# Masks, normalizations and feature steps shared between VectorE and GpSimd, with a new table of order, engines and buffers

## The chip, the cores and the metric

The kernel runs on one core of a Trainium2 chip, in one launch. A core has five engines that run their own instruction streams and wait for each other through semaphores: TensorE (PE in the profile, with its weight loads as PEld), ScalarE (ACT), VectorE (DVE), GpSimd (POOL) and SyncE (SP), which here only issues DMAs. The metric is the device time of one execution in microseconds, as the median of several runs.

## The reference

A sequence of 2048 tokens with 512 channels runs through four blocks, two of a kind, each with its own normalization and residual:

```python
x = x + _A_ref(_layernorm(x), A_wq, A_wk, A_wv, A_wo, A_beta)
x = x + _B_ref(_layernorm(x), B_wqkv, B_w_phi, B_wo)
x = x + _A_ref(_layernorm(x), A_wq, A_wk, A_wv, A_wo, A_beta)
x = x + _B_ref(_layernorm(x), B_wqkv, B_w_phi, B_wo)
```

Block A has 32 heads of 16 channels and works in 4 segments of 512 tokens. Inside a segment it is causal softmax attention; beside it stands a linear memory of the earlier segments, and a gate `g` per head mixes the two:

```python
phi = lambda t: jnp.where(t > 0, t + 1.0, jnp.exp(t))
logits = einsum('bhqd,bhkd->bhqk', qs, ks) * scale + mask
a_dot = einsum('bhqk,bhkd->bhqd', softmax(logits), vs)
a_mem = einsum('bhld,bhde->bhle', phi(qs), M) / (einsum('bhld,bhd->bhl', phi(qs), z)[..., None] + 1e-06)
o = g * a_mem + (1.0 - g) * a_dot
M = M + einsum('bhld,bhle->bhde', phi(ks), vs);  z = z + phi(ks).sum over l
```

Block B is linear attention without a mask: queries and keys go through a small matrix per head, then softmax of it and of its negative are the features; keys and values of all 2048 tokens are summed into one matrix per head before the queries are multiplied with it.

## The kernel before

The sequence is held in SBUF as `X`, 16 tiles of 128 tokens. The two pairs of layers (`L` = 0, 1) run one after the other. Block A goes by segment `s` (four tiles each): `a_proj` makes queries, keys and values of a segment, `a_att` does the attention of two tiles at a time, `out_proj` adds the result to `X`; then the tiles are normalized again and `b_keys` adds the segment's part of block B's sums. After the fourth segment `b_query` runs over the four groups of tiles, and in layer 0 the next layer's normalization and projections follow each group.

What the change touches is this:

- `ln` normalizes one tile: statistics (`bn_stats`, L590, and `bn_aggr`, L591, on DVE), the inverse root (L598 and L600 on POOL, or on ACT for the first four tiles), and then the normalized tile `xn`, `(X - mean) * rstd`, 128x512. `xn` is on DVE at L611, or on DVE (L607) or ACT (L608) where the tile may go either way. SP then transposes it by DMA (L383), or PE does (`tpe`).
- `a_proj` copies the keys out of PSUM (`Kev`, L374 on ACT or L375 on DVE) and writes four masked copies of them (`Km`, L703), 128x1024 each: a mask keeps one head in four and sets the others to zero, so that a matmul over 64 rows, which hold four heads, sees one head at a time. There are 64 such masks in the program, all on DVE. The score matmuls of block A read them as tile `pQ`.
- `phi` makes the feature map: ACT takes the exponential, L649 takes `max(x, 0) + 1`, L650 the minimum of the two. There are 24 of each, the latter two on DVE.
- Two kinds of additions, L882 (attention plus memory) and L1093 (the two halves of block B's result), are on DVE or POOL by the table.

Nothing of the order is decided when the program is built. Every operation is recorded in a graph with the engines that may do it and a cost in ns for each. A packed table, `ORDER`, holds three lists: the sequence of all 2748 operations, the engine of each, and the buffer of each of the 1498 tiles. `place` unpacks it and `emit` writes each engine's stream in that sequence, with the waits that the data and the reuse of buffers need. An engine never takes its operations in another order. So the costs in the code are notes for whoever made the table; they do nothing at run time.

Of the kernel before, what the change touches and what calls it, by code (L numbers as in the profile page):

```python
# [10 lines left out]
ALU = mybir.AluOpType  # L11
# [301 lines left out]
class Kernel:  # L313
# [149 lines left out]
    def T(self, pool, cls):  # L463
        return Tile(pool, cls)
# [122 lines left out]
    def ln(self, t, xT, flex=False, pe=False, root="pool"):  # L587
# [14 lines left out]
        xn = self.T(self.p1, "xn")  # L602
        if flex:
# [3 lines left out]
            self.g.op({"dve": (323, lambda e: e.tensor_scalar(xn.t[:], self.X[:, t, :], self.mv[:, t, 0:1], rs, op0=ALU.subtract, op1=ALU.mult)),  # L607
                       "act": (700, lambda e: e.activation(xn.t[:], self.X[:, t, :], ACT.Identity, scale=rs, bias=nb))},  # L608
                      [R("X", t), R("mv", t), R("rstd", t), R("nb", t)], [xn], label="xn", port=True)
        else:  # L610
          v(lambda e: e.tensor_scalar(xn.t[:], self.X[:, t, :], self.mv[:, t, 0:1], self.rstd[:, t:t + 1],  # L611
                                    op0=ALU.subtract, op1=ALU.mult), 300,
          [R("X", t), R("mv", t), R("rstd", t)], [xn], label="xn", port=True)
# [30 lines left out]
    def phi(self, dst, src):  # L644
# [4 lines left out]
        v(lambda e: e.tensor_scalar(dst.t[:], src.t[:], 0.0, 1.0, op0=ALU.max, op1=ALU.add), 335, [src[0], src[1]], [dst], label="phmax", port=True)  # L649
# [32 lines left out]
    def a_proj(self, L, s):  # L682
# [7 lines left out]
        for hp in range(2):  # L690
# [11 lines left out]
            for sl in range(4):  # L702
# [3 lines left out]
                self.g.op({"dve": (400.0, fn)}, [KT[0], KT[1], R("m4")], [KM[sl]], label="Km", port=True)  # L706
# [567 lines left out]
```

## Time and profile before

| | |
|---|---|
| time, median of 3 runs | 462.59 us (462.41 to 462.62) |
| span of the profiled execution | 461.2 us |
| instructions with a recorded time: PE, DVE, ACT, POOL | 11716, 807, 542, 160 |
| one mask, one normalization, one feature step (L649) on DVE | 476, 417, 423 ns |
| one inverse root on POOL (L598 and L600) | 272 and 587 ns |

The span runs from the first to the last instruction; the time of a run is 1.4 us more. A row of the groups of instructions gives line, engine, operation, tiles, shape and count, then the busy time of them all and the mean of one, then the idle time of the engine just before them with what ended it. Instructions of one engine overlap a little, so the busy time of a group can be less than count times mean. A row of the waits reads "engine, tile, line <- engine, tile, line that ended the wait: us in total, times, longest".

### The profile page before, as it was taken

The numbers are of one execution on the slowest core, as the hardware profiler recorded it, in microseconds if no ns is written. First come the engines' busy times: TensorE is split into PE (matmuls) and PEld (weight loads), VectorE is DVE, ScalarE is ACT, GpSimd is POOL, SyncE is SP. The second block draws the span as 40 slices with busy tenths as digits, with TensorE's granted clock in tenths as the row PEclk, the third lists the DMA queues.
The fourth block names the chain that finished last, engine by engine and source line by source line (L and its number), as shares of the span: only waits on it lengthen the run. The fifth ranks groups of instructions, "written<-read, shape, count | busy, mean of one in ns | idle before, by whom it ended". The sixth has DMA issues, their size and how long they took to land.

```text
span 461.2 us, 25354 instructions
## 1 busy us (share of the span) xinstructions
PE 437.7 (95%) x11716; PEld 295.6 (64%) x11716; DVE 416.2 (90%) x807; ACT 420.3 (91%) x542; POOL 80.1 (17%) x160
## 2 busy tenths in 40 slices
PE   8989899899999999998899999999999999998896
PEld 4456667667776776675456677677677677666553
DVE  6989998898889999898999899998899889998896
ACT  4999999899999998789699999999999999878991
POOL 2402021101221211102532031130221023110020
PEclk9999999999999999999999999999999999999999
DMA  8554642552233322100243443264113321200357
GB/s 247 127 150 80 127 63 37 75 96 54 50 46 54 46 40 36 37 3 4 48 54 78 71 85 72 49 96 61 26 39 49 50 39 27 48 14 1 50 121 180
DMA packets 90058, 30.37 MB, mean 66 GB/s; under 512 B 76640, under 2 KB 89952, under 8 KB 89952
## 3 DMA queue, kind: packets, MB, share of 16 engines
q1 hardware_dynamic: 89520, 28.48, 33.3%
q8 instruction: 92, 1.51, 1.4%
q10 hardware_dynamic: 432, 0.27, 0.2%
q14 instruction: 14, 0.11, 0.1%
HBM read 6.32 MB, written 2.10 MB: 18 GB/s over the span
## 4 chain that ended last, share of the span: by engine, by line
PE 48%; ACT 40%; DVE 6%; DMA 3%; issue 2%; SPq 0%
PE D L356 31%; ACT p L366 21%; PE D L341 15%; ACT pF L366 13%; ACT pE L366 5%; DMA p<-p 2%; PE D L662 2%; DVE X L926 1%; DMA X<-in_A_x_dram 1%; DVE p L1090 1%; DVE p L375 1%; DVE stats L590 1%; ACT pS L366 1%; DVE p L611 0%; DVE pK L375 0%
## 5 line engine op out<-in xcount | busy, mean ns | idle before, releaser
L366 ACT ACTIVATE p<-D 128x1024 bf16<-128x1024 f32 (+2 forms) x224 | 216.0, 1004 | 13.5 <-PE D L356 9.7
L366 ACT ACTIVATE pF<-D 128x896 bf16<-128x896 f32 x128 | 116.7, 940 | 2.8 <-PE D L341 2.5
L341 PE MATMUL D<-pK,pQ 64*128 64x256 bf16 (+3 forms) x1536 | 112.9, 243 | 4.1 <-ACT pF L366 1.0
L341 PEld LDWEIGHTS D<-pK,pQ 64*128 64x128 bf16 x1536 | 55.2, 94 | 40.7 <-ACT pF L366 5.4
L341 PE MATMUL D<-pV,pF 64*128 64x34 bf16 x1024 | 73.8, 175 | 0.4 <-ACT p L366 0.4
L341 PE MATMUL D<-pW,pF 64*128 64x34 bf16 x1024 | 71.3, 175 | 0.0
L341 PEld LDWEIGHTS D<-pV,pF 64*128 64x128 bf16 x1024 | 55.3, 93 | 2.3 <-ACT p L366 0.7
L341 PE MATMUL D<-pV,p 64*128 64x34 bf16 x1024 | 53.3, 176 | 0.3 <-issue 0.2
L366 ACT ACTIVATE pE<-D 128x768 bf16<-128x768 f32 x64 | 52.3, 831 | 1.4 <-PE D L341 1.0
L341 PEld LDWEIGHTS D<-pW,pF 64*128 64x128 bf16 x1024 | 51.9, 93 | 0.9
L341 PE MATMUL D<-pW,p 64*128 64x34 bf16 x1024 | 52.1, 176 | 0.0
L598 POOL TENSOR_SCALAR rstd<-mv 128x1 f32<-128x1 f32 x60 | 16.1, 272 | 205.9 <-DVE mv L591 205.5
L341 PEld LDWEIGHTS D<-pV,p 64*128 64x128 bf16 x1024 | 47.0, 93 | 3.3 <-issue 0.9
L341 PE MATMUL D<-tri,two 64*128 64x128 bf16 (+1 forms) x384 | 46.7, 234 | 0.4 <-issue 0.4
L341 PEld LDWEIGHTS D<-pW,p 64*128 64x128 bf16 x1024 | 45.2, 93 | 1.3
L590 DVE BATCH_NORM_STATS2 stats<-X 128x6 f32<-128x512 bf16 x64 | 42.9, 680 | 3.0 <-DMA X<-in_A_x_dram 2.5
L341 PE MATMUL D<-pV,pE 64*128 64x34 bf16 x512 | 44.9, 175 | 0.4 <-issue 0.4
L926 DVE TENSOR_TENSOR X<-X,D 128x1024 bf16<-128x1024 bf16 (+1 forms) x36 | 39.4, 1095 | 5.7 <-PE D L356 5.0
L341 PE MATMUL D<-pW,pE 64*128 64x34 bf16 x512 | 42.5, 175 | 0.1
L985 DVE TENSOR_REDUCE pS<-p 128x64 f32<-128x1024 bf16 (+1 forms) x36 | 38.8, 1088 | 1.8 <-ACT p L366 1.8
L375 DVE CAST p<-D 128x512 bf16<-128x512 f32 x48 | 31.1, 683 | 6.3 <-PE D L356 6.1
L356 PE MATMUL D<-WB_o,p 64*128 64x512 bf16 (+1 forms) x288 | 33.0, 353 | 2.7 <-issue 1.3
(115 smaller groups left out, 988.9 us busy)
## 6 DMA issues: line engine op xcount, KB each, us to landing
pW<-pV SPq DMA_DIRECT2D x16, 136.0 KB, 3.1
out_dram<-X SPq DMA_DIRECT2D x7, 256.0 KB, 2.8
X<-in_A_x_dram SPq DMA_DIRECT2D x3, 512.0 KB, 6.1
pX<-in_B_wqkv_dram SPq DMA_DIRECT2D x3, 512.0 KB, 4.6
p<-p SPq DMA_TRANSPOSE x76, 2.8
pX<-p SPq DMA_TRANSPOSE x54, 3.2
WA_k<-in_A_wk_dram SPq DMA_DIRECT2D x2, 256.0 KB, 6.3
WA_q<-in_A_wq_dram SPq DMA_DIRECT2D x2, 256.0 KB, 7.0
```

Of the source, the lines that this page charges most:

```text
L341: ins = e.matmul(out_ap, lhsT, rhs, start=st, stop=sp, tile_position=(basep(lhsT), basep(out_ap)))
L356: ins = e.matmul(out_ap, lhsT[64 * hf:64 * hf + 64], rhs[64 * hf:64 * hf + 64], start=k == 0 and i == 0, stop=k == 1 and i == len(lists[hf ...
L366: return self.g.op({"act": (dur, lambda e: e.activation(out_ap(), in_ap(), func, scale=scale))}, reads, writes, opens, label=label)
L375: "dve": ((340 if fast else n / 0.96 + 65), lambda e: e.tensor_copy(out_ap(), in_ap()))}
L590: v(lambda e: e.bn_stats(self.stats[:, t, :], self.X[:, t, :]), 602, [R("X", t)], [R("st", t)], label="bn")
L598: v(lambda e: e.tensor_scalar(rs, self.mv[:, t, 1:2], LN_EPS, None, op0=ALU.add), 170, [R("mv", t)], [R("rstd", t)], eng="pool", label="rstd")
L662: ins = e.matmul(D.t[c0:, r0 * 8:r0 * 8 + n], r[:, c0:], ones(r, n), start=True, stop=True, tile_position=(r0, c0))
L926: self.v(lambda e: e.tensor_tensor(X(), X(), src(), ALU.add), 65 + 512 * n / 0.96, pr + xr, xr, label="res")
L985: fn = lambda e, sgn=sgn, eo=eo, Z=Z, n=n: e.tensor_reduce(Z.t[:, 0:64 * n].rearrange("p (k s h) -> p k s h", k=n, s=2)[:, :, sgn, :], eo( ...
L1090: v(lambda e, N=N, Tm=Tm, w=w, shape=shape: e.tensor_tensor(shape(Tm.t[:]), shape(N.t[:]), w(), ALU.mult), 1131, [N, AB[(0, 0)], AB[(0, 1) ...
```

## The change

Three kinds of operations, which were bound to DVE (the normalization to DVE or ACT in some tiles), may also be on POOL. The table is a new one. The costs noted for two of them are 323 for 300 and 396 for 400 ns.

```diff
         xn = self.T(self.p1, "xn")
+        nrm = lambda e: e.tensor_scalar(xn.t[:], self.X[:, t, :], self.mv[:, t, 0:1], rs, op0=ALU.subtract, op1=ALU.mult)
         if flex:
...
-            self.g.op({"dve": (323, lambda e: e.tensor_scalar(xn.t[:], self.X[:, t, :], self.mv[:, t, 0:1], rs, op0=ALU.subtract, op1=ALU.mult)),
+            self.g.op({"dve": (323, nrm), "pool": (700.0, nrm),
                        "act": (700, lambda e: e.activation(xn.t[:], self.X[:, t, :], ACT.Identity, scale=rs, bias=nb))},
...
-          v(lambda e: e.tensor_scalar(xn.t[:], self.X[:, t, :], self.mv[:, t, 0:1], self.rstd[:, t:t + 1],
-                                    op0=ALU.subtract, op1=ALU.mult), 300,
-          [R("X", t), R("mv", t), R("rstd", t)], [xn], label="xn", port=True)
+            self.g.op({"dve": (323, nrm), "pool": (700.0, nrm)}, [R("X", t), R("mv", t), R("rstd", t)], [xn], label="xn", port=True)
...
-        v(lambda e: e.tensor_scalar(dst.t[:], src.t[:], 0.0, 1.0, op0=ALU.max, op1=ALU.add), 335, [src[0], src[1]], [dst], label="phmax", port=True)
+        fn = lambda e: e.tensor_scalar(dst.t[:], src.t[:], 0.0, 1.0, op0=ALU.max, op1=ALU.add)
+        self.g.op({"dve": (335.0, fn), "pool": (1100.0, fn)}, [src[0], src[1]], [dst], label="phmax", port=True)
...
-                self.g.op({"dve": (400.0, fn)}, [KT[0], KT[1], R("m4")], [KM[sl]], label="Km", port=True)
+                self.g.op({"dve": (396.0, fn), "pool": (1100.0, fn)}, [KT[0], KT[1], R("m4")], [KM[sl]], label="Km", port=True)
...
 ORDER = """
-c-rlG1GFYtlWpMm8fDwIZQHhO+qP}n=q}rAn`L%ab=S-MZdXt9|9jTVd+W_wli$7hWu9{~V#kghk(u{qfQFD5k^n<eNCu6dF*JchkQ&lJIzUJPDIpbPg!E7oN<u9FC<w
...
+c-qZ*1JotQ7Vbv*H^#PY+qP}nwr$(Cl?;MGGDyY~XPC?c<H@}4^UuV2_rAOCUF-EZr@O1VYUA5`e^tE>Kn7?CsUZ!dg+`D9QbJ;A3{4;vq=$kafB>N+6at2tPznk|5hw~tASu*>rqB#3
...
```

Unpacked, both tables hold the same 2748 operations and 1498 tiles. What changes its engine:

```
operation                           engine         count (of)
mask (Km, L703)                     DVE to POOL    45 (64)
normalization (xn, L607/L611)       DVE to POOL    45 (60 on DVE)
normalization (xn, L608)            ACT to POOL 1, ACT to DVE 1 (4 on ACT)
feature step (phmax, L649)          DVE to POOL    8 (24)
addition (L882)                     DVE to POOL 5, POOL to DVE 5 (24)
addition (L1093)                    DVE to POOL 6, POOL to DVE 1 (26)
evacuation of PSUM (L374/L375)      ACT to DVE 9, DVE to ACT 7
small set-up fills                  POOL to DVE 2, DVE to POOL 1
operations on DVE                   807 to 708
operations on POOL                  156 to 259
operations on ACT                   544 to 540
```

PE and SP keep all of theirs. The sequence is shuffled locally on all engines: half of PE's operations stay within one place of where they were, nine in ten within six. 1163 of the 1498 tiles have another buffer. Of SP's loads at the start, the one of X's last four tiles (12 to 15) goes from place 15 to place 6, and that of tiles 8 to 11 from place 7 to place 14, just ahead of the first transposes. At the end, one of the stores that stood ahead of SP's last transposes moves behind them.

More of the change, by code (lines that the diff above doesn't have):

```diff
@@ L1234 @@
[L1234 to L1235 removed]
+c-qZ*1JotQ7Vbv*H^#PY+qP}nwr$(Cl?;MGGDyY~XPC?c<H@}4^UuV2_rAOCUF-EZr@O1VYUA5`e^tE>Kn7?CsUZ!dg+`D9QbJ;A3{4;vq=$kafB>N+6at2tPznk|5hw~tASu*>rqB#3
+LUSk$m7q4%fifVWER=(~&;nXQD`*Xsp$fEtw$KjRLkH*xouD&xfvQjpibFLh0rj9f<OKuup#oHg8W03$;4I{UC^!ZAp(}KQ2B6^rT!ij03^GCl#03XEpcf>9WH1wk!z@tH6Z*qB_y|6R
```

110 lines of the change are left out of this document (52 added, 58 removed).

## The prediction

> **What bounds the kernel now.** I read the page's first part, then the same busy times by stage (the windows view), because a share over the whole span is a mean over stages with different limits. A row of that view has the stretch, its length, the busy time (and the count of instructions) of PE, PEld, DVE, ACT and POOL, the granted clock, the DMA share and the GB/s.
>
> ```profile
> PE 437.7 (95%) x11716; PEld 295.6 (64%) x11716; DVE 416.2 (90%) x807; ACT 420.3 (91%) x542; POOL 80.1 (17%) x160
> 0.00:30.00 30.00, 26.79 (x360) 14.12 (x360) 24.49 (x66) 21.86 (x35) 8.89 (x32) 1.00 0.72 197
> 30.00:180.00 150.00, 143.62 (x4374) 102.18 (x4368) 136.62 (x255) 147.19 (x179) 21.55 (x40) 1.00 0.37 62
> 180.00:207.00 27.00, 26.93 (x574) 18.73 (x570) 24.40 (x47) 20.49 (x27) 3.20 (x8) 1.00 0.10 19
> 207.00:228.00 21.00, 17.54 (x543) 10.30 (x537) 18.87 (x40) 18.72 (x34) 8.13 (x12) 1.00 0.12 25
> 228.00:240.00 12.00, 12.00 (x146) 5.61 (x140) 11.90 (x22) 9.46 (x14) 4.32 (x5) 1.00 0.24 49
> 240.00:390.00 150.00, 147.91 (x4316) 104.64 (x4314) 137.25 (x268) 148.29 (x183) 27.27 (x52) 1.00 0.36 58
> 390.00:424.00 34.00, 34.00 (x720) 23.17 (x716) 31.64 (x55) 28.30 (x36) 4.31 (x9) 1.00 0.11 22
> 424.00:461.20 37.20, 28.87 (x738) 16.90 (x732) 31.03 (x59) 26.03 (x40) 2.43 (x2) 0.98 0.50 109
> ```
>
> The reader is to see that DVE, the engine that the change relieves, is the tight one almost nowhere. In the two attention stages (30 to 180 and 240 to 390, together 300 us) ACT is idle for 150 - 147.19 = 2.8 us and 150 - 148.29 = 1.7 us. In 180 to 207, 228 to 240 and 390 to 424 (73 us) PE is idle for 0.1 us in all. That leaves the start, the turn between the layers (207 to 228) and the end.
>
> Next, what PE and ACT wait for. These are the rows between 30 and 390 us in which PE's idle time ends on DVE (four more rows, one of 0.4 us at L1087 and three of 0.2 us at L375, are left out), and the one in which ACT's does:
>
> ```profile
> PE D L341 <- DVE p L1060: 1.0, 1, 1.0
> PE D L341 <- DVE p L607: 0.4, 1, 0.4
> PE D L341 <- DVE X L926: 0.4, 1, 0.4
> ...
> PE D L341 <- DVE WB_k L375: 0.2, 1, 0.2
> ACT pS L366 <- DVE pS L1061: 1.2, 1, 1.2
> ```
>
> With those four they add up to 4.2 us, and of the operations that move, one row alone is there: a normalization (L607), 0.4 us. No row names a mask (pQ, L703) or the first step of the feature map (L649). So what moves is mostly not what anyone waits for. At the turn (213 to 227) the chain of waits does run through DVE, but nearly all of it through operations that stay there (multiply L1090, residual L926, statistics L590); the normalization L607 has 3.0%, 0.4 us:
>
> ```profile
> by line: DVE p L1090 32.9%; DVE X L926 24.6%; DVE stats L590 17.6%; DVE p L1087 6.9%; DVE p L375 4.3%; DVE mv L591 3.8%; DVE p L607 3.0%; DVE pS L1065 2.9%; DVE p L1060 2.4%; DVE nb L605 2.3%; issue 1.9%; PE D L341 1.4%; DVE pS L1061 1.2%
> ```
>
> **The change, part by part.** The rows that price it:
>
> ```profile
> L703 DVE TENSOR_SCALAR pQ<-p,m 128x1024 bf16<-128x1024 bf16 x64 | 29.4, 476 | 0.5 <-ACT p L374 0.3
> L611 DVE TENSOR_SCALAR p<-X,mv,rstd 128x512 bf16<-128x512 bf16 x44 | 18.1, 417 | 1.7 <-POOL rstd L600 1.4
> L649 DVE TENSOR_SCALAR p<-p 128x1024 bf16<-128x1024 bf16 x12 | 5.0, 423 | 0.1
> 451.17 0.42 DVE L1093 TENSOR_TENSOR p<-p 128x512 bf16<-128x512 bf16 x1
> L374 ACT ACTIVATE p<-D 128x512 bf16<-128x512 f32 x28 | 15.9, 597 | 6.7 <-PE D L356 4.6 <-PE D L341 1.9
> L608 ACT ACTIVATE p<-X,nb,rstd 128x512 bf16<-128x512 bf16 x4 | 3.2, 800 | 0.0
> L518 POOL TENSOR_SCALAR_AFFINE_SELECT H<-H 128x8 f32<-128x8 f32 x1 | 0.2, 192 | 0.1
> L523 POOL TENSOR_SCALAR_AFFINE_SELECT ident<-ident 128x128 bf16<-128x128 bf16 x1 | 0.3, 292 | 0.1
> L598 POOL TENSOR_SCALAR rstd<-mv 128x1 f32<-128x1 f32 x60 | 16.1, 272 | 205.9 <-DVE mv L591 205.5
> L1093 POOL TENSOR_TENSOR p<-p x10: 1147/1154/1531, 215.2 to 443.5; 128x512 bf16<-128x512 bf16 x10
> ```
>
> *Off DVE.* The unpacked table moves 45 of 64 masks, 45 normalizations and 8 of 24 feature steps from DVE to POOL, and a net 5 additions. By busy time over count: 45 x 29.4/64 = 20.7, 45 x 18.1/44 = 18.5, 8 x 5.0/12 = 3.3, 5 x 0.42 = 2.1 us. Evacuations trade places (9 from ACT to DVE, 7 back) and one normalization comes from ACT: about +1.7 us. DVE loses 42.9 us and would stand near 373.
>
> *Onto POOL.* No row shows these three operations there. From below: one input streams from 8 to 128 elements in 292 - 192 = 100 ns, 0.83 ns an element, and the same operation on one element takes 272 ns; so 272 + 0.83 x 1024 = 1.12 us for a mask and 0.70 us for a normalization. From above: 512 elements with two inputs take 1.15 us, so 2.3 and 1.15 us. I take the lower ones, since these operations have one tensor input. POOL gains 45 x 1.12 + 46 x 0.70 + 8 x 1.12 + 5 x 1.15 = 97 us (from above 180) and stands near 177 us of 461: it does not become the bound either way.
>
> *What hides them.* A mask takes 0.6 us longer and a normalization 0.3; the rows of waits above say that nobody waited for them. Behind a normalization stands SP's transpose, and behind that the rest of SP's queue:
>
> ```profile
> SPq L383 <- DVE p L611: 36.8, 11, 10.1
> ```
>
> SP already sits up to 10.1 us there with no loss to PE, so 0.3 us more is covered; without that cover it would be 46 x 0.3 = 14 us. I cost this at 0 and keep 0 to +2.
>
> *ACT.* In the two attention stages six evacuations leave ACT and four come: 2 x 15.9/28 = **-1.1 us** on the engine that is busy 99% of that time. The bounds are 0 and -1.1 - 4.5 (all of ACT's idle time there closing too).
>
> *The turn.* One of four normalizations (800 ns) goes from ACT to POOL, but the chain there is DVE work that stays: 0, bounds -0.8 and +0.5.
>
> *The start.* The table also reorders SP's loads: the load of X's last quarter goes from behind the first four transposes to sixth place, and X's third quarter from seventh to just before the transposes.
>
> ```profile
> 14.75 6.36 SPq L383 DMA_TRANSPOSE pX<-p  x4
> 21.16 0.58 SPq L474 DMA_DIRECT2D X<-in_A_x_dram  x1
> 26.23 0.69 DVE L590 BATCH_NORM_STATS2 stats<-X 128x6 f32<-128x512 bf16 x1 [1.53 <-DMA X<-in_A_x_dram]
> 2.00:14.00 12.00, 11.41 (x161) 6.01 (x161) 9.71 (x31) 6.56 (x16) 3.62 (x12) 1.00 0.98 298
> ```
>
> DVE's idle 1.53 us ends on that late load, so it goes. In its place 4.8 MB now stand ahead of the end of X's third quarter, which at 298 GB/s lands at 2 + 16 = 18 us, about when DVE gets to its statistics: 0 to 1.5 us. I take -1.5 + 0.5 = **-1.0 us**, bounds -1.5 and +1.0.
>
> *The end.* One store fewer stands ahead of the last transposes on SP, but an addition ahead of the last one is POOL's (1.15 for 0.42 us):
>
> ```profile
> 453.12 1.19 SPq L383 DMA_TRANSPOSE p<-p  x1
> 439.57 0.57 SPq L387 DMA_DIRECT2D out_dram<-X  x1
> ```
>
> That addition started at 451.17 on DVE (quoted above); on POOL it ends at 451.17 + 1.15 = 452.3, before SP gets there: **-0.4 us** for the store, bounds -0.6 and +0.7.
>
> *A port that both engines want.* This is the term that speaks against the change.
>
> ```profile
> 130.82 1.16 POOL L882 TENSOR_TENSOR p<-p 128x512 bf16<-128x512 bf16 x1 [5.98 <-DVE p L795]
> 383.74 0.68 DVE L1007 TENSOR_TENSOR pT<-p,pT 128x1024 bf16<-128x1024 bf16 x1
> 383.91 1.53 POOL L882 TENSOR_TENSOR p<-p 128x512 bf16<-128x512 bf16 x1 [8.02 <-DVE p L795]
> 384.92 1.07 DVE L1007 TENSOR_TENSOR pT<-p,pT 128x1024 bf16<-128x1024 bf16 x1
> 220.70 1.22 DVE L1090 TENSOR_TENSOR p<-D,pS 128x1024 bf16<-128x1024 f32 x1
> 220.80 2.35 POOL L1093 TENSOR_TENSOR p<-p 128x512 bf16<-128x512 bf16 x2 [0.23 <-DVE nb L605]
> ```
>
> The first L1007 (0.68 us) runs into POOL's addition, which takes 1.53 instead of 1.16; the second starts while 0.52 us of that addition are left and takes 0.39 longer. Whoever comes second waits. L1090, which reads PSUM, and POOL's additions run side by side at full speed (1.22 us, and 2.35 us for two), so only DVE work that reads SBUF alone is hit. The Trainium skill has the rule without a price (GPSIMD Engine Reference, Key points: VectorE's SBUF interfaces are shared, and contention comes with two-port modes or two SBUF inputs); the trace agrees, with 1.07 for 0.68 us, and the rule by itself, each overlap a wait, is the port rival below. Price: after the change DVE keeps about 145 large operations that read SBUF alone (32 L1007, 24 L650, 20 L1087, 19 masks, 16 normalizations, 16 feature steps, 18 additions); POOL is on large ones for 45 x 1.12 + 46 x 0.70 + 8 x 1.12 + 26 x 1.15 = 121 us, 26% of the span. Each meets one at 0.26 and loses about 0.36 (half of a mean POOL operation of 1 us, less the 0.52 - 0.39 = 0.13 that the row above did not lose): 145 x 0.26 x 0.36 = 14 us of DVE, so DVE would show about 387 busy. DVE is 6% of the chain (below), mostly at the turn, in L1090 and L926, which read PSUM, and L590, which reads one tensor: I take 3% of the 14 us, **+0.4 us**; bounds 0 and +4 (some 30% of the 14 us on the path).
>
> ```profile
> PE 48%; ACT 40%; DVE 6%; DMA 3%; issue 2%; SPq 0%
> ```
>
> **Sum.** -1.1 - 1.0 - 0.4 + 0.4 = -2.1 us on the profiled execution's span of 461.2, so 459.1. The time runs 462.59 - 461.2 = 1.4 us above the span, so 460.5.
>
> **Rivals.** Two runs of this kernel can be told apart from about 0.2%, which is 0.9 us.
> - *The slack is used everywhere.* With 43 us less on DVE everything reaches PE and ACT earlier, and the 4.5 us that ACT is idle in the attention stages close, with the 4.2 us of waits on DVE partly among them. For it: three engines at 90% jam each other. Against it: ACT's idle time there ends on PE. -2.1 - 3.5 gives 457.
> - *It does nothing that counts.* ACT and PE hold their stages as now, the gain at the start is given back to the later quarter of X: 462.3.
> - *Slower: the port.* POOL's masks, 1.12 us each, stand before DVE's reads at places where an evacuation or a weighted value is queued behind them in DVE's order and PE waits for that. It decides as soon as more than 2.5 of the 14 us fall on the path (gain used up), and at 4 to 6 us it gives 464.5 to 466. For it: the 1.07 us above. Against it: PE and ACT wait on DVE for only 4.2 us in 360.
> - *Slower: the start.* X's third quarter lands 2 us after DVE wants it, and evacuations queue behind it: 463.8.
>
> **How the numbers follow.** Forecast (459 to 461.6) 0.37, slack used everywhere 0.12, nothing 0.24, port 0.20, start 0.07. That is faster 0.49, same 0.24, slower 0.27. Predicted: 460.5. The range takes in most of the slack case and most of the port's: 457.0 to 465.0; the forecast's own range is 459.0 to 461.6.
>
> **What would show it.** DVE near 387 us busy, POOL near 177, mask 1.1 to 1.4 us and normalization 0.7 to 0.9 on POOL; L1007 and L650 above 0.69 us on average (some near 1.1); ACT near 418 busy, still 98% and more in both attention stages; DVE's idle time on X's load gone, or moved to another quarter. The prediction is wrong if masks take 2 us (PE would wait for pQ), if the chain's DVE share grows past 10%, or if ACT's share in the attention stages falls: then PE was kept waiting by something new.

## The result, and the profile after

The changed kernel takes 545.24 us (median of 4 runs, 541.94 to 549.37), the kernel before 462.50 beside it. The ratio is 1.1786, with a 95% interval of 1.1700 to 1.1872: **slower by 18%**, 83 us, where a gain of 2 us was predicted. The profiled execution has a span of 540.2 us, which the notes below refer to.

First the page of the changed kernel: busy times, the granted clock in 40 slices, and the chain that ended last by engine.

```profile
PE 456.9 (85%) x11716; PEld 300.5 (56%) x11716; DVE 402.1 (74%) x708; ACT 422.9 (78%) x538; POOL 342.9 (63%) x263
PEclk9998989899997999899899989889799999999999
PE 34%; POOL 31%; DVE 14%; ACT 7%; DMA 7%; issue 4%; SPq 2%; DVEq 0%; POOLq 0%
```

POOL is busy for 343 us, not 177, and 31% of the chain now runs through it, where it had no share. No engine is full any more: PE fell from 95% to 85% and ACT from 91% to 78%. An engine that is busy 63% of the time and yet holds the others up doesn't lack capacity; its results come late.

The stages, in two stretches of 160 us that lie inside the two attention stages (columns as in the prediction):

```profile
40.00:200.00 160.00, 139.81 (x4038) 96.24 (x4039) 117.40 (x195) 137.56 (x165) 119.21 (x80) 0.95 0.29 52
290.00:450.00 160.00, 133.87 (x3770) 92.64 (x3770) 110.10 (x189) 128.32 (x155) 120.79 (x79) 0.95 0.30 46
```

ACT had 147.19 of 150 us in the first attention stage. Now it has 137.56 of 160, or 86%, and 80% in the second. The loss is spread over both stages; no single stall makes it.

The groups of the three operations on POOL, with the mean ns of one behind the busy time:

```profile
L703 POOL TENSOR_SCALAR pQ<-p,m 128x1024 bf16<-128x1024 bf16 x45 | 131.2, 2921 | 27.5 <-DVE p L375 13.4 <-DVE mv L591 10.3 <-ACT p L374 3.7
L603 POOL TENSOR_SCALAR p<-X,mv,rstd 128x512 bf16<-128x512 bf16 x46 | 99.3, 2161 | 7.0 <-DVE mv L591 3.3 <-DVE nb L606 0.9
L648 POOL TENSOR_SCALAR p<-pK 128x1024 bf16<-128x1024 bf16 x6 | 21.9, 3651 | 1.4 <-DVE pK L375 1.1
```

A mask takes 2.92 us where 1.12 was assumed, a normalization 2.16 for 0.70, a feature step 3.65 for 1.12. In the timeline of POOL one sees what that does to small operations that stand in the same queue (start, duration, operation, and in brackets what it waited for):

```profile
305.26 5.69 POOL L703 TENSOR_SCALAR pQ<-p,m 128x1024 bf16<-128x1024 bf16 x2 [1.96 <-ACT p L374]
311.01 3.70 POOL L648 TENSOR_SCALAR p<-pK 128x1024 bf16<-128x1024 bf16 x1
314.79 0.23 POOL L598 TENSOR_SCALAR rstd<-mv 128x1 f32<-128x1 f32 x1
314.97 1.08 POOL L600 TENSOR_TENSOR rstd<-rstd,mhalf 128x1 f32<-128x1 f32 x2
316.05 2.85 POOL L703 TENSOR_SCALAR pQ<-p,m 128x1024 bf16<-128x1024 bf16 x1
318.89 2.08 POOL L603 TENSOR_SCALAR p<-X,mv,rstd 128x512 bf16<-128x512 bf16 x1
```

An inverse root of 0.23 us comes behind 9.4 us of masks and a feature step, and the normalization that needs it stands behind one more mask on the same engine. The waits of the changed kernel name the consequences (us in total, times, longest):

```profile
POOL rstd L598 <- DVE mv L591: 68.7, 21, 11.1
ACT p L366 <- PE D L341: 41.9, 25, 4.5
...
PEld D L341 <- POOL pQ L703: 18.3, 6, 5.1
PE D L341 <- POOL pQ L703: 16.8, 6, 4.9
...
DVE p L650 <- POOL p L648: 11.5, 3, 6.1
...
DVE nb L606 <- POOL rstd L600: 8.5, 4, 4.3
...
PE D L356 <- DMA pX<-p: 6.6, 6, 3.0
```

PE waits for masks (pQ) and for late transposes, which stand behind late normalizations; DVE waits for POOL's feature steps and inverse roots. ACT then waits for PE: 41.9 us in the row on L341, which had 2.6 before. And POOL's own wait for statistics fell from 205.5 to 68.7 us: most of the slack that it had before is used up by its own work.

### The profile page after: what moved, and what is told of

It reads as the page before. It is cut to its first block, busy times and chain, and to the rows that moved or that the text cites. A ratio compares the mean times of both kernels' runs of the same rounds, so it can differ in the third digit from the quotient of the medians.

```text
span 540.2 us, 25363 instructions
## 1 busy us (share of the span) xinstructions
PE 456.9 (85%) x11716; PEld 300.5 (56%) x11716; DVE 402.1 (74%) x708; ACT 422.9 (78%) x538; POOL 342.9 (63%) x263
## 4 chain that ended last, share of the span: by engine, by line
PE 34%; POOL 31%; DVE 14%; ACT 7%; DMA 7%; issue 4%; SPq 2%; DVEq 0%; POOLq 0%
PE D L356 23%; POOL pQ L703 13%; PE D L341 11%; POOL p L603 9%; POOL p L648 5%; ACT p L366 4%; DMA pX<-p 4%; POOL rstd L600 3%; DVE X L926 2%; ACT pF L366 2%; DVE p L375 2%; DMA p<-p 2%; DMA WA_k<-in_A_wk_dram 2%; DVE stats L590 1%; SPq L474 1%
## 5 line engine op out<-in xcount | busy, mean ns | idle before, releaser
L366 ACT ACTIVATE p<-D 128x1024 bf16<-128x1024 f32 (+2 forms) x224 | 215.3, 994 | 63.1 <-PE D L341 41.9
L703 POOL TENSOR_SCALAR pQ<-p,m 128x1024 bf16<-128x1024 bf16 x45 | 131.2, 2921 | 27.5 <-DVE p L375 13.4
L341 PE MATMUL D<-pK,pQ 64*128 64x256 bf16 (+3 forms) x1536 | 116.4, 249 | 29.6 <-POOL pQ L703 16.8
L366 ACT ACTIVATE pF<-D 128x896 bf16<-128x896 f32 x128 | 114.9, 930 | 10.1 <-PE D L341 9.4
L603 POOL TENSOR_SCALAR p<-X,mv,rstd 128x512 bf16<-128x512 bf16 x46 | 99.3, 2161 | 7.0 <-DVE mv L591 3.3
L341 PEld LDWEIGHTS D<-pK,pQ 64*128 64x128 bf16 x1536 | 57.8, 96 | 69.4 <-POOL pQ L703 18.3
L341 PE MATMUL D<-pV,pF 64*128 64x34 bf16 x1024 | 73.9, 176 | 2.8 <-DVE MS L756 2.3
L341 PE MATMUL D<-pW,pF 64*128 64x34 bf16 x1024 | 71.0, 176 | 0.1
L598 POOL TENSOR_SCALAR rstd<-mv 128x1 f32<-128x1 f32 x60 | 15.5, 261 | 69.1 <-DVE mv L591 68.7
L341 PEld LDWEIGHTS D<-pV,pF 64*128 64x128 bf16 x1024 | 55.9, 93 | 4.8 <-DVE MS L756 2.5
L1093 POOL TENSOR_TENSOR p<-p 128x512 bf16<-128x512 bf16 x15 | 18.3, 1222 | 58.7 <-DVE p L1087 34.6
L341 PE MATMUL D<-pV,p 64*128 64x34 bf16 x1024 | 53.4, 176 | 0.2 <-ACT pF L366 0.2
L341 PEld LDWEIGHTS D<-pW,pF 64*128 64x128 bf16 x1024 | 51.4, 93 | 1.3 <-issue 0.2
L341 PE MATMUL D<-pW,p 64*128 64x34 bf16 x1024 | 51.8, 176 | 0.0
L356 PE MATMUL D<-WB_k,pX 64*128 64x512 bf16 (+1 forms) x288 | 36.5, 379 | 14.9 <-issue 7.8
L341 PEld LDWEIGHTS D<-pV,p 64*128 64x128 bf16 x1024 | 47.7, 93 | 2.4 <-ACT pF L366 0.5
L341 PE MATMUL D<-tri,two 64*128 64x128 bf16 (+1 forms) x384 | 47.3, 237 | 1.0 <-issue 1.0
L341 PEld LDWEIGHTS D<-pW,p 64*128 64x128 bf16 x1024 | 45.5, 93 | 1.6
L341 PE MATMUL D<-pV,pE 64*128 64x34 bf16 x512 | 44.2, 176 | 0.0
```

Source lines behind the costliest of these rows:

```text
L341: ins = e.matmul(out_ap, lhsT, rhs, start=st, stop=sp, tile_position=(basep(lhsT), basep(out_ap)))
L356: ins = e.matmul(out_ap, lhsT[64 * hf:64 * hf + 64], rhs[64 * hf:64 * hf + 64], start=k == 0 and i == 0, stop=k == 1 and i == len(lists[hf ...
L366: return self.g.op({"act": (dur, lambda e: e.activation(out_ap(), in_ap(), func, scale=scale))}, reads, writes, opens, label=label)
L598: v(lambda e: e.tensor_scalar(rs, self.mv[:, t, 1:2], LN_EPS, None, op0=ALU.add), 170, [R("mv", t)], [R("rstd", t)], eng="pool", label="rstd")
L603: nrm = lambda e: e.tensor_scalar(xn.t[:], self.X[:, t, :], self.mv[:, t, 0:1], rs, op0=ALU.subtract, op1=ALU.mult)
L703: fn = lambda e, KM=KM, KT=KT, sl=sl: e.tensor_scalar(KM.t[:, :, sl % 2, :, 64 * (sl // 2):64 * (sl // 2) + 64], KT.t[:].rearrange("p (j h ...
```

## Experiments

Times are medians, ratios are to the kernel before, run on the same chip; its median was 460.3 to 462.5 us. What was expected of a run stands as it was put on record before it, word for word.

### Whose fault: the engines or the new sequence?

Three kernels keep the new sequence and buffers and put operations back on DVE: all three kinds in e1, as below, only `'Km'` in e2, only `'xn'` in e3.

```diff
+        raw = bytearray(raw)
+        for o in self.ops:
+            if o.label in BACK and ENGS[raw[2 * n + o.id]] == "pool":
+                raw[2 * n + o.id] = ENGS.index("dve")
+        raw = bytes(raw)
...
+BACK = ('Km', 'xn', 'phmax')
```

> The changed kernel's sequence and buffers, with the 45 masks, 46 normalizations and 8 feature steps put back on DVE. Theory 'durations' (the three operations take 2.85, 2.08 and 3.64 us on GpSimd where 1.12, 0.70 and 1.12 were assumed, and what waits for them is late): the loss goes, 455 to 470 us. Theory 'sequence' (the new order and buffers are bad by themselves): it stays, 535 to 550 us. Theory 'port' (the two engines block each other) also gives 455 to 470 here; it is told apart from 'durations' by the run that measures the operations alone.

> The changed kernel with the 45 masks alone put back on DVE; normalizations and feature steps stay on GpSimd. Theory 'durations': the masks hold 13% of the chain of waits (70 us of 540), the other two 14%, and taking one away lets the others come forward, so about half of the 80 us goes: 490 to 515 us. Theory 'sequence': 535 to 550 us.

> The changed kernel with the 45 normalizations from DVE and the one from ACT put on DVE; masks and feature steps stay on GpSimd. Theory 'durations': the normalizations hold 9% of the chain (49 us), so a third to a half of the 80 us goes: 500 to 520 us. Theory 'sequence': 535 to 550 us.

e1: 540.91 us, 1.1737 (1.1648 to 1.1826). e2: 524.44, 1.1374 (1.1318 to 1.1429), between its two expectations. e3: 558.1 and 567.1 us in its two runs, too far apart for an interval, and both above what either theory expected. With everything back on DVE nothing is won, although POOL is nearly idle again. The waits of e1:

```profile
POOL rstd L603 <- DVE mv L596: 284.8, 40, 20.2
...
PE D L361 <- DMA pX<-p: 28.4, 11, 5.1
...
PE D L346 <- DVE pQ L708: 15.7, 8, 3.1
```

PE now waits for the same two things, masks and transposes, out of DVE's queue. So it can't be said that POOL's durations alone are to blame, nor that the sequence is bad in itself: it was tried with other engines than it has in the table. Two kernels cross the tables the other way. e6 has the sequence and buffers of after with the whole engine list of before:

```diff
+        old = zlib.decompress(base64.b85decode("".join(ENGINES.split())))
+        raw = raw[:2 * n] + old[2 * n:3 * n] + raw[3 * n:]
```

e5 has the table of before, with these three kinds on the engines that they have in after:

```diff
+        for o in self.ops:
+            if o.label in ("Km", "xn", "phmax"):
+                raw[2 * n + o.id] = new[2 * n + o.id]
```

> The sequence and the buffers of the kernel before, with the 99 masks, normalizations and feature steps on GpSimd as the new table has them; all else as before. Theory 'sequence' (the new order or buffers lose the time by themselves, the engines do not matter): 460 to 475 us. Theory 'durations' (operations of 2.85, 2.08 and 3.64 us on GpSimd come too late): 500 to 570 us, since this order gives GpSimd no lead at all.

> The new sequence and buffers, with every operation on the engine that it had before, evacuations and additions too. Theory 'sequence': 530 to 550 us, as with the three kinds alone put back (541). Theory 'durations' in its simple form (what is slow is what GpSimd does): 460 to 475 us; the run with the three kinds put back speaks against that already. A third theory, 'fit' (the sequence is made for durations, and any others upset it): 520 to 550 us.

e5: 550.26 us, 1.1948 (1.1800 to 1.2096). e6: 549.02, 1.1921 (1.1768 to 1.2074). In e6 every operation is on the engine, and in the form, that it has in the fast kernel; the sequence and the buffers alone differ, and it loses 19%. **One list sets the order of every engine's queue, and with the whole of the other engine list it does badly**; such a crossed pair loses as much as the change itself. e1, e5 and e6 show that. They do not tell the order from the buffers, and they leave open what the new pair would do if its durations were right.

### What POOL needs for these operations

m1 runs the forms by themselves on POOL, three or four of each, and then some beside DVE; below the mask (L66), the normalization (L72), the feature step (L74), a copy (L78) and two multiplies of two tensors (L80, L82):

```python
                e.tensor_scalar(km(KMt, sl), x4, s0, None, op0=ALU.mult)
...
                e.tensor_scalar(new(H), X[:, 0:512], s0, s1, op0=ALU.subtract, op1=ALU.mult)
...
                e.tensor_scalar(new(BF), X[:], 0.0, 1.0, op0=ALU.max, op1=ALU.add)
...
                e.tensor_copy(new(BF), X[:])
...
                e.tensor_tensor(new(BF), X[:], cw[:], ALU.mult)
...
                e.tensor_tensor(new(BF), X[:], c[:, 0:1].to_broadcast([128, 1024]), ALU.mult)
```

> Computes none of the reference: GpSimd runs each form of the operations three or four times with VectorE idle, then masks and two-input multiplications beside VectorE. Theory 'durations': the mask takes 2.85 us alone (strided or contiguous), the normalization 2.08, the feature step 3.64, and little more beside VectorE. Theory 'port': 1.1, 0.7 and 1.1 us alone, and 2.1 to 3.6 only beside VectorE. A two-input multiplication of 1024 elements is expected at 2.2 us by the 1.15 us for 512, so below the mask with one input. VectorE beside GpSimd: by 'port' its 0.69 us multiplications wait up to a whole GpSimd operation.

Its timeline (start, duration of the whole group, operation, count):

```profile
4.25 11.30 POOL L66 TENSOR_SCALAR KM<-X,c 128x1024 bf16<-128x1024 bf16 x4 [3.83 <-DVE X L51]
15.52 8.48 POOL L68 TENSOR_SCALAR o<-X,c 128x1024 bf16<-128x1024 bf16 x3
23.98 4.64 POOL L70 TENSOR_SCALAR o<-X,c 128x512 bf16<-128x512 bf16 x3
28.61 6.19 POOL L72 TENSOR_SCALAR o<-X,c 128x512 bf16<-128x512 bf16 x3
34.76 10.82 POOL L74 TENSOR_SCALAR o<-X 128x1024 bf16<-128x1024 bf16 x3
...
53.72 3.00 POOL L78 COPY o<-X 128x1024 bf16<-128x1024 bf16 x3
56.69 6.26 POOL L80 TENSOR_TENSOR o<-X,cw 128x1024 bf16<-128x1024 bf16 x3
62.90 5.59 POOL L82 TENSOR_TENSOR o<-X,c 128x1024 bf16<-128x1024 bf16 x3
```

With DVE silent a mask takes 11.30 / 4 = 2.83 us, strided or not (8.48 / 3 = 2.83), a normalization 2.06, a feature step 3.61. The durations are the operations' own, not the port's. And the order of the forms is not what one tensor input suggests: the one-input multiply takes 2.83 us, the two-tensor multiply 6.26 / 3 = 2.09, with a repeated column 1.86, a copy 1.00. The Trainium skill (GPSIMD Engine Reference, Engine selection) says of elementwise work on GpSimd that one-input operations run at roughly line rate and two-input ones about twice slower than on VectorE; the rows here disagree for this form, and DVE's mask takes 476 ns.

The second half of m1 keeps DVE busy beside POOL with operations that take 0.68 us (two tensors, L58) and 0.47 us (one tensor, L60) undisturbed. Two places, POOL's operation and the DVE operation that it holds up:

```profile
86.64 3.87 POOL L91 TENSOR_SCALAR o<-X,c 128x1024 bf16<-128x1024 bf16 x1
87.80 1.52 DVE L58 TENSOR_TENSOR o<-dta,cw 128x1024 bf16<-128x1024 bf16 x1
```

```profile
99.76 2.29 POOL L93 TENSOR_TENSOR o<-X,cw 128x1024 bf16<-128x1024 bf16 x1
100.00 2.33 DVE L60 TENSOR_SCALAR o<-dta,c 128x1024 bf16<-128x1024 bf16 x1
```

Beside the one-input multiply DVE's multiplications of L58 are held up once, for 0.84 us, and the others run at 0.68 us meanwhile, while POOL's own operation takes 3.87 us for 2.83. Beside the two-tensor multiply DVE's operation waits to its end.

e8 uses the cheaper form for the 45 masks in the changed kernel:

```diff
-                self.g.op({"dve": (396.0, fn), "pool": (1100.0, fn)}, [KT[0], KT[1], R("m4")], [KM[sl]], label="Km", port=True)
+                ttm = lambda e, KM=KM, KT=KT, sl=sl: e.tensor_tensor(
+                    KM.t[:, :, sl % 2, :, 64 * (sl // 2):64 * (sl // 2) + 64], KT.t[:].rearrange("p (j h k) -> p j h k", j=8, h=2),
+                    self.m4[:, sl:sl + 1][:, :, None, None].to_broadcast([128, 8, 2, 64]), ALU.mult)
+                self.g.op({"dve": (396.0, fn), "pool": (1100.0, ttm)}, [KT[0], KT[1], R("m4")], [KM[sl]], label="Km", port=True)
```

> The changed kernel with GpSimd's 45 masks as a multiplication of two tensors, the second one the mask column repeated; alone this form took 1.86 us where the mask with a scalar pointer took 2.83. Theories 'durations' and 'fit': 45 x 1 us less on GpSimd takes 10 to 30 us off: 515 to 535 us. Theory 'sequence': 540 to 550 us.

e8: 532.50 us, 1.1562 (1.1455 to 1.1670). A third off the masks returns 2%; their cheaper form also holds DVE up more, which is busy for 420.1 us instead of 402.1.

### The changed kernel with the durations that were assumed

In e7 POOL's masks and normalizations become copies and its feature steps fills, which happen to take what the prediction assumed. In e9 and e13 the first two segments of layer 0 keep the copies. From segment `s` = 2 on, e9 has two one-element powers for a mask and one for a normalization, which take about as long as the copies but hardly touch SBUF (its feature steps stay fills); in e13 each of the three kinds is a fill of one element and takes next to nothing. The edit of the normalization in e7, and what stands for an operation in e9 and in e13:

```diff
+        cpx = lambda e: e.tensor_copy(xn.t[:], self.X[:, t, :])
...
-            self.g.op({"dve": (323, nrm), "pool": (700.0, nrm)}, [R("X", t), R("mv", t), R("rstd", t)], [xn], label="xn", port=True)
+            self.g.op({"dve": (323, nrm), "pool": (700.0, cpx)}, [R("X", t), R("mv", t), R("rstd", t)], [xn], label="xn", port=True)
```

```diff
+            ins = e.tensor_tensor(self.scr[:, c:c + 1], self.ones8[:, 0:1], self.mhalf[:], ALU.pow)
```

```diff
+            ins = e.memset(self.scr[:, c:c + 1], 1.0)
```

> The changed kernel with sequence, buffers and engines as they are, but GpSimd's masks and normalizations replaced by plain copies and its feature steps by a fill with 1, so masking, normalization and feature map are partly left out; a copy of 1024 took 1.0 us alone, which is near the 1.10 and 0.70 us noted in the code. Theory 'fit' and theory 'durations': with the durations that the sequence was made for, it runs at 450 to 470 us. Theory 'sequence': 530 us or more all the same.

> Like the run with copies (479 us), but past the first two segments each copy on GpSimd is replaced by one or two powers of a single element (0.57 us each) that touch none of the tiles: a mask costs 1.1 us, a normalization 0.57, a feature step is a fill. Masks and normalizations are left out there. GpSimd's queue is as full as with copies, but it hardly reads SBUF. If the 18 us that the copies still lose come from the port (VectorE's stalls add up to 17 us there): 460 to 470 us. If they come from the sequence or the buffers: 475 to 482 us.

> The changed kernel's sequence, buffers and engine list; from the second segment on each of GpSimd's added key masks, normalizations and feature steps is a fill of one element (about 0.1 us); the masks, normalizations and feature steps are left out there. Queue-time theory: the 12 to 13 us that were left in e9_pow (474.3) are time in GpSimd's in-order queue, so with nearly no time in it the kernel comes to 458 to 466. Sequence theory: the new order and buffers themselves cost it, whatever GpSimd's operations take: 470 to 476.

The groups of e7 on POOL:

```profile
L707 POOL COPY pQ<-p 128x1024 bf16<-128x1024 bf16 x45 | 48.3, 1091 | 41.9 <-DVE p L375 37.7 <-DVE nb L607 2.3 <-ACT p L374 1.9
L604 POOL COPY p<-X 128x512 bf16<-128x512 bf16 x46 | 32.2, 706 | 10.7 <-DVE nb L607 9.0
L650 POOL MEMSET p<- 128x1024 bf16 x8 | 7.9, 986 | 21.6 <-DVE p L375 13.3 <-DVE pK L375 8.3
```

e7: 479.08 us, 1.0402 (1.0317 to 1.0488). e9: 474.32, 1.0304 (1.0256 to 1.0353). e13: 472.27, 1.0267 (1.0215 to 1.0319). So (1.1786 - 1.0402) x 461.5 = 64 of the 83 us go with the durations, and 12 us stay even where POOL's new work takes next to nothing. e7 and e9 come out between their expectations, e13 within that of the sequence theory. POOL is busy for 172.0, 169.7 and 107.4 us in the three. So 4.5 us go with the copies' traffic (e7 to e9) and 1.7 us with 62 us of POOL's time (e9 to e13), though neither step is clear of noise by itself. What the 12 are is not settled: the new order and buffers, or the copies in the first two segments.

### Is it the time on POOL, or DVE stalling beside it?

e7 changes both at once, for a copy touches SBUF for a shorter time too. e17 and e18 keep the durations and leave out the traffic: each of these operations, from segment 2 on, is a chain of one-element powers and fills.

A mask, a normalization and a feature step are `spend(4, 4)`, `spend(3, 3)` and `spend(6, 0)` in e17, `spend(5, 4)`, `spend(4, 0)` and `spend(7, 0)` in e18, with

```diff
+    def spend(self, e, k, j):
+        for n in range(k + j):
+            c = self.nscr % 96
+            self.nscr += 1
+            o = self.scr[:, c:c + 1]
+            ins = e.tensor_tensor(o, self.ones8[:, 0:1], self.mhalf[:], ALU.pow) if n < k else e.memset(o, 1.0)
+        return ins
```

> The changed kernel; from the third segment on each of GpSimd's added masks, normalizations and feature steps is a chain of one-element powers (0.6 us) and fills (0.12 us) that takes as long as the operation (4 + 4 for a mask, 2.9 us; 3 + 3 for a normalization, 2.2 us; 6 powers for a feature step, 3.6 us) and hardly touches SBUF; the masks, normalizations and feature steps are left out there. If the 64 us between the changed kernel (ratio 1.179) and e7_copies (1.040) are time in GpSimd's queue: 525 to 545. If they are VectorE's stalls beside longer operations, as in e14 and e16: 472 to 490.

> As e17_time_only (514.2, ratio 1.112), whose chains came out shorter than the operations that they stand for (about 2.3, 1.7 and 3.2 us by its timeline, and GpSimd 303 us busy for 343): now 5 powers and 4 fills for a mask, 4 powers for a normalization, 7 powers for a feature step, which comes to 2.85, 2.1 and 3.7 us; the same work is left out. If the gap between e17 and the changed kernel (1.179) was those shorter durations: 535 to 547. If it was VectorE's stalls (5.5 us in e17, 15.6 in the changed kernel): 512 to 522, hardly more than e17.

e17: 514.23 us, 1.1122 (1.1075 to 1.1169), with POOL busy for 303 us, between its two expectations. e18 gets the durations right:

```profile
PE 459.3 (85%) x11716; PEld 303.6 (56%) x11716; DVE 392.2 (73%) x708; ACT 421.9 (79%) x538; POOL 341.0 (63%) x703
```

POOL stands at 341.0 us for the changed kernel's 342.9, and the time is 543.48 us, 1.1796 (1.1731 to 1.1862), for 1.1786. Adding up, for each DVE instruction that ran beside a long POOL operation, what it took above the median of its undisturbed fellows gives 4.9 us of stalls in e18 and 15.6 in the changed kernel. Two thirds of the stalls are gone and, within the intervals, nothing is won; whereas the 38 us by which POOL is busier than in e17 cost (1.1796 - 1.1122) x 461.5 = 31 us. **The 64 us are time in POOL's queue.**

### Slack of one's own, and the place in the queue

The other runs use the table of before and move operations to POOL without touching the sequence: only the 45 masks (e11), only the 46 normalizations (e12), and 23 masks that in the trace of before were done at least 10 us ahead of the first exponential that needs them, in the cheaper form (e10).

`SLACK` holds these 23; the loop over `BEHIND`, 13 of them, is in e14 to e16 only, which come below:

```diff
+        for i in SLACK:
+            assert self.ops[i].label == "Km"
+            raw[2 * n + i] = ENGS.index("pool")
...
+        for m, p in BEHIND:
+            o = self.ops[m]
+            order.remove(o)
+            order.insert(order.index(self.ops[p]) + 1, o)
```

> The sequence and buffers of the kernel before, with the 45 masks on GpSimd (2.85 us each) and nothing else moved. With all 99 operations moved it took 550. If the masks hold up their own readers and the queue: 510 to 535 us.

> The sequence and buffers of the kernel before, with the 46 normalizations on GpSimd (2.08 us each) and nothing else moved. If the normalizations lengthen the path from a residual to the next projection by 1.7 us a tile and that path is what the stages wait for: 490 to 520 us; if there is slack on it, as the waits of the kernel before said: 461 to 470 us.

> The kernel before, with only those 23 masks on GpSimd that are done 10 us or more ahead of the first exponential that needs them, in the two-tensor form (1.86 us). If a moved operation costs nothing as long as its own reader has slack: 459 to 462 us, no gain either, since VectorE was not what the stages waited for. If GpSimd's queue behind the masks matters (the inverse roots of the layer norms come later): 464 to 480 us.

e11: 501.71 us, 1.0899 (1.0858 to 1.0940), less of a loss than expected. e12: 483.79, 1.0510 (1.0437 to 1.0583), between its two expectations. e10: 482.01, 1.0475 (1.0441 to 1.0508), 2 us above the higher of its two ranges, although each mask had slack. POOL's timeline in e10, and the one of before at the same place:

```profile
115.65 1.89 POOL L711 TENSOR_TENSOR pQ<-p,m 128x1024 bf16<-128x1024 bf16 x1 [18.57 <-DVE p L380]
117.50 1.61 POOL L890 TENSOR_TENSOR p<-p 128x512 bf16<-128x512 bf16 x1
119.08 0.22 POOL L603 TENSOR_SCALAR rstd<-mv 128x1 f32<-128x1 f32 x1
```

```profile
107.22 1.32 POOL L882 TENSOR_TENSOR p<-p 128x512 bf16<-128x512 bf16 x1 [23.78 <-DVE p L878]
```

In before the addition (L882 there, L890 here) ran at 107.22. In e10 it runs at 117.50, because a mask that comes ahead of it in the sequence waits for its keys until 115.65. The mask has time; what stands behind it doesn't. SP's transposes wait for that addition, and PE waits for them:

```profile
119.14 1.29 SPq L388 DMA_TRANSPOSE p<-p  x1
PE D L361 <- DMA p<-p: 4.0, 1, 4.0
```

In before that transpose went out at 108.57, and no row of e10's waits has PE waiting for a mask on POOL. The windows of e10 show where that ends (stretch, its length, PE, PEld, DVE, ACT and POOL busy, then the granted clock):

```profile
115.00:120.00 5.00, 4.92 (x192) 3.95 (x183) 4.55 (x9) 5.00 (x8) 3.65 (x3) 1.00 0.02 7
120.00:125.00 5.00, 1.02 (x8) 0.40 (x10) 2.43 (x3) 1.64 (x2) 4.79 (x5) 0.82 0.39 93
125.00:130.00 5.00, 5.00 (x68) 2.62 (x66) 1.53 (x2) 2.16 (x3) 2.10 (x2) 0.50 0.57 106
130.00:135.00 5.00, 5.00 (x192) 4.07 (x189) 4.63 (x10) 5.00 (x7) 1.13 (x2) 0.99 0.15 31
```

PE stands idle for 4 us and then works at half the clock. The Trainium skill (TensorE: Matmul & The Clock Gate, What's actually happening) has the rule: after an idle window of about 3.4 us the array falls to half its clock until it has been busy for as long. These rows agree on the drop, with 0.82 and then 0.50; the clock is back only at about 130, after more than 5 us of matmuls.

e14 moves 13 of these masks in the sequence behind the operations that they had held up. e15 then replaces 21 of the 23 by a fill of one element, and e16 by three one-element powers, about as long as a mask but without the traffic (the other two, in the first segments, stay).

> e10_slack (the order of before, 23 masks with at least 10 us of slack on GpSimd as two-tensor multiplications, 482.0) with 13 of the 23 masks moved, in the sequence, behind the GpSimd operation (finished-input addition or rstd) that in before ran earlier in time but stands later in the sequence. Queue theory: what cost e10 was the operations that stood behind a waiting mask in GpSimd's in-order queue, so the loss of 19.5 us falls to below a third: 461 to 468. Slack theory (the masks themselves come too late for their readers, or VectorE's stalls beside them): nothing or little changes, 475 to 485.

> e14_behind (471.8), with those of its GpSimd masks that lie behind the second segment replaced by a fill of one element (about 0.1 us); those masks are left out. If the 11 us that e14 still loses are the masks' own time on GpSimd (the queue behind them, and VectorE's stalls beside them, 16 us in e14 against 1.4 before): 459 to 464. If they come from the order itself (the masks standing in GpSimd's queue, waiting for key evacuations, with the inverse roots behind them, however short they are): 466 to 472.

> e15_behind_fill (462.3, the ratio to before 1.001) with three one-element powers (about 0.6 us each, 1.8 us together, hardly touching SBUF) in place of each fill, so that GpSimd spends the time of a mask but VectorE does not stall beside it; the same masks are left out. If e14's loss (2.5%) is VectorE's stalls (16 us there, 1.4 in e15): 461 to 464, as e15. If it is the masks' time in GpSimd's queue: 468 to 473, as e14.

e14: 471.75 us, 1.0252 (1.0203 to 1.0302), between its two expectations: half of e10's loss was the place in the queue (DVE's stalls, added up as above, are the same in both, 16.0 and 15.9 us). e15: 462.27, 1.0010 (0.9988 to 1.0032). e16: 462.23, 1.0014 (0.9994 to 1.0035). So the other half isn't the masks' time, which e16 keeps; it goes with the masks' traffic, and DVE's stalls beside them go with it. DVE's and POOL's timelines in e14:

```profile
147.05 1.90 POOL L715 TENSOR_TENSOR pQ<-p,m 128x1024 bf16<-128x1024 bf16 x1
147.07 2.16 DVE L894 TENSOR_TENSOR p<-p 128x512 bf16<-128x512 bf16 x1
```

An addition of 0.42 us starts 0.02 us after a mask on POOL and ends 0.28 us after it: it waited for all of it. The Trainium skill (Trainium Architecture — The Big Picture, What this means for kernel authors) calls the pair of ports that the two share an exclusive lock and not a split of bandwidth; the rows agree here, where POOL's operation reads two tensors, and m1's agree less where it reads one (held up for 0.84 of 3.87 us). In e16 the stalls are 1.2 us, in before 1.4. The pages of e14, then of e16:

```profile
PE 439.3 (94%) x11716; PEld 296.1 (63%) x11716; DVE 422.8 (90%) x784; ACT 422.1 (90%) x542; POOL 124.6 (27%) x183
```

```profile
PE 438.9 (95%) x11716; PEld 295.6 (64%) x11716; DVE 407.9 (89%) x784; ACT 420.5 (91%) x542; POOL 119.8 (26%) x225
```

DVE has 23 masks fewer than before in both. In e14 it is busier than before all the same (422.8 for 416.2 us): the stalls put back more than the 23 x 0.476 = 11 us that left. Taking the traffic away wins (1.0252 - 1.0014) x 461.5 = 11 us of time. And in e16 DVE is relieved of 8 us at no price, and the time does not fall. No run here beats the kernel before.

## Why the prediction was wrong

The failed step is the one called "Onto POOL", and behind it "What hides them". They are not the whole miss: e7, with about the durations that were assumed, still takes 479.08 us, above the range's end at 465.

- **Onto POOL: the size.** 97 us were taken, 180 given as the upper end; the added work is 343 - 80 = 263. The slope came from two selections of 8 and 128 columns, 0.83 ns an element, and was carried to a multiply by a per-partition scalar on 1024 columns, since both have one tensor input. That form takes 2.83 us, above the upper end too, which was the two-input addition scaled up. That POOL "does not become the bound either way" went by its share of the span; at a share of 63% it has 31% of the chain. The prediction's own condition, "The prediction is wrong if masks take 2 us", came true, with DVE's chain share at 14% and ACT at 86% and 80% in the attention stages besides. e7 and e18 show that this size makes 64 of the 83 us.
- **What hides them: costed at 0, kept to +2 us.** The reading was that nobody waits for a mask or a normalization, so a longer one is covered. The waits of before say how late an operation's own reader is. They do not say what stands behind it in its new engine's queue. e10 is the case by itself: masks with 10 us of slack, placed in POOL's queue without a new order, cost 4.75%, and half of it went when 13 of them were moved behind others. In the new order the cover does hold at the assumed sizes (e9 is 1.7 us above e13, within the intervals); at the real sizes it is used up, which is the 64 us.
- **What bounds the kernel: right.** DVE is the tight engine almost nowhere; e15 and e16 take 8 us off it and gain nothing (1.0010 and 1.0014). The rival "It does nothing that counts" is what these two come to, with the old order and 23 masks; no run has all 99 operations off DVE at no price. The chances should have followed this reading: with nothing to gain on DVE, the whole gain in the forecast came from edits beside the change.
- **The port: the size right by luck, the price wrong.** 14 us of stalls were forecast for DVE, and 15.6 - 1.4 = 14.2 came, but not by that sum. It took POOL to be on large operations for 121 us, 26% of the span, at 1 us each; it was on them for 291 us, 54%, at 2.3 us each, and with these the same sum gives some 80 us (its 18 additions left on DVE are 24 in the trace, which adds little). Against that, m1 has L58 held up beside a one-input multiply for 0.84 us only. Put down to the POOL operation that each overlaps most, the stalls are 8.9 us beside the 45 masks, 4.6 beside the 26 additions, 1.6 beside the feature steps and 0.5 beside the 46 normalizations. Two errors cancelled. The rows foreseen near 0.69 us are there in the changed kernel:

```profile
L1007 DVE TENSOR_TENSOR pT<-p,pT 128x1024 bf16<-128x1024 bf16 x32 | 23.1, 729 | 1.3 <-ACT p L374 0.8
L650 DVE TENSOR_TENSOR p<-p 128x1024 bf16<-128x1024 bf16 x24 | 17.6, 736 | 13.3 <-POOL p L648 11.5 <-ACT p L366 1.6
```

  The durations of all DVE instructions together fall from 464.8 to 436.8 us, 28.0 for the 28.9 forecast, by the same luck; DVE's busy time falls by half of that only, to 402 for 387, since instructions that stand apart no longer overlap at their ends. Of the stalls, 3% were put on the path. In the changed kernel they cost nothing that e18 can show, as POOL is later still; but where POOL isn't late (e14), 14.5 us of stalls go with a loss of 11 us. The chain's share of 6% for DVE was no measure of that: DVE was relieved for nothing, yet three quarters of its delay counts there.
- **ACT: not borne out.** ACT is busy for 422.9 us in the changed kernel, 2.6 more and not 1.1 less. In e13, with POOL's new work next to nothing, it is 418.6, 1.7 less, but with PE late nothing comes of it.
- **The start: half right.** The 1.53 us on the late load at 26.23 are gone, as forecast, and X's third quarter is not waited for. But two waits at 3.5 and 6.7 us take their place, so that nearly nothing is won (DVE's waits for X's loads in before, then the two of the changed kernel, 1.40 for 1.01 us and a new one of 0.92):

```profile
DVE stats L590 <- DMA X<-in_A_x_dram: 2.5, 2, 1.5
```

```profile
3.54 1.29 DVE L590 BATCH_NORM_STATS2 stats<-X 128x6 f32<-128x512 bf16 x2 [1.40 <-DMA X<-in_A_x_dram]
6.67 0.70 DVE L590 BATCH_NORM_STATS2 stats<-X 128x6 f32<-128x512 bf16 x1 [0.92 <-DMA X<-in_A_x_dram]
```

- **The end and the turn** can't be read off, being behind 80 us of other loss.

What stays open is the 12 us of e13 (2.67%): the sum there should have been about -2 us by the prediction's other terms, and no run splits the new order from the new buffers or from the copies in the first two segments.

## What to carry to other kernels

Before work is moved to another engine, time that very form of instruction there; a row of another operation with the same number of inputs was wrong by a factor of 2.5 to 3.3. An operation's slack toward its own reader doesn't make it free: read who stands behind it in the in-order queue that it joins, and what it delays on an engine that shares its ports. And where the relieved engine isn't what the others wait for, the best case is no change, so that every risk on the other side is a loss.

## What was not expected of the hardware

- On POOL a one-input multiply by a per-partition scalar (2.83 us for 128x1024, bf16) is slower than a two-tensor multiply (2.09) or one with a repeated column (1.86), and a second operation adds (2.06 for 1.55 us at 512 columns, 4.64 / 3 against 6.19 / 3 above).
- A DVE operation that reads SBUF alone waits for the whole of a two-tensor POOL operation that started just before it: 2.16 us for 0.42 in e14, 2.33 for 0.47 in m1. Beside a one-input multiply on POOL, m1's two-tensor multiplications are held up for 0.84 us of 3.87 only, and POOL's operation gets 1 us longer.
- In e10, 4 us without matmuls cost PE more than the 4 us: the next 5 us ran at a granted clock of 0.50. In the changed kernel the mean granted clock is 0.962, and PE's busy time is 456.9 us for 437.7 with the same matmuls.
